# Sparse attention and a mixture of experts on one core: scores and products with v at two points of a unit's stretch in place of one

## The chip, the cores and the metric

The kernel runs on 1 core of one Trainium2 chip. The metric is the device time of one execution in microseconds (us).

## The reference

A batch of 4 sequences of 768 tokens with 8 heads of 64 passes through block-sparse attention (blocks of 32; each block of queries sees its neighbours, the first and last block, and 3 sampled blocks; the first and last block of queries see everything). Its output, 3072 tokens of 512, passes through a mixture of 4 experts.

```python
# attention
scores = scale * np.matmul(q, k.transpose(0, 1, 3, 2))
scores = np.where(mask, scores, -1000000000.0)
scores = scores - np.max(scores, axis=-1, keepdims=True)
attn = np.exp(scores)
attn = attn / (np.sum(attn, axis=-1, keepdims=True) + 1e-09)
out = np.matmul(attn, v)
# experts: x (3072, 512), w1 (4, 512, 1024), w2 (4, 1024, 512)
p = domain_probs / (domain_probs.sum(-1, keepdims=True) + 1e-09)
for e in range(E):
    h = np.maximum(x @ w1[e], 0.0)
    out += p[:, e:e + 1] * (h @ w2[e])
```

## The kernel before

Attention of batch 0 runs first, by itself. After that one stream of expert products (`experts()`, a generator) fills TensorE, and attention of batches 1, 2 and 3 ("later attention") is threaded into it: batch b's attention runs while the experts work on batch b-1. The experts go on after the last attention.

*The experts.* The four experts' hidden layers are 8 chunks of 512. Matrix products are made of seven smaller ones (the scheme of Strassen and Winograd; in batch 0 the second layer is plain). Each number is split in two fp32r parts, and three partial products give the accuracy of fp32. A first-layer product (`first`, `first7`, matmuls at L754, tiles `w` and `v`) is 6 matmuls of 128x128 by 128x384, and so is a second-layer product of the later batches (`second7`, L991, tiles `u` and `v`); batch 0's second layer (`second`, L827, tile `po`) has 3 matmuls of 128x512. Their results are taken out of PSUM by VectorE and ScalarE. Of these steps the text names L813, L842, L869, L892 and L902 (VectorE's sums and the scaling by the expert's weight `pb`, tile `ha`). The sum into the output tile `tot` is at L1001. `hidden` makes the second layer's operands: a cast on ScalarE (L914) and a subtraction on POOL (L915).

*Attention in units.* A batch has N = 16 units: 4 of kind Edge (first and last block of queries, each over two halves of the keys) and 12 of kind Group (6 groups of up to 4 query blocks, each for two halves of the heads). A unit has four steps:
- `S`: the scores, 32 or 64 small matmuls of 64x32 tiles (16 for an Edge; L355, L362 and L433, tiles `s` and `sw`) into two PSUM buffers, then on VectorE the mask and the row maximum (L372; for an Edge L444 to L449), and on ScalarE the exponential (L374; L451) into `p`;
- `T`: 6 or 8 transposes of `p` on TensorE (L383, L462) into the same two PSUM buffers that S uses, each half copied out to `pt` by ScalarE (L385, L463);
- `A`: the products with v, 32, 48 or 64 small matmuls of 128x32 tiles (L396, L474, tile `o`), then on VectorE the normalisation (L402 to L404 into `xg`; for an Edge L481 to L489 into `xe`);
- `X`: after every second unit, the transposes of the finished rows (L415, L495, tiles `x` and `xt`), in the one PSUM buffer that A uses too, and ScalarE's copy into the expert's input (L417, L497).

`copy_k` brings the sampled key blocks together (L158, POOL and ScalarE), `load_q` and `load_v` fetch q and v (SyncE's queue, and POOL's indirect loads at L213).

*The order.* It is written out by hand: each engine executes its instructions in the order in which the program issues them. `drive(until)` takes products from the stream until the sum of their planned costs (`T1` = 0.975 us for a 384-column product, `T2` = 0.6475 for one of batch 0's second layer) reaches `until`. Batch b's later attention has `N + 1` equal stretches of planned length `per` between two fixed points of the stream:

```python
LEAD, TAIL = 32.0, 25.0
start = base[b - 1] + LEAD
per = (base[b] - TAIL - start) / (N + 1)
```

With `base` of 0, 235.5, 440.2 and 660.6 this gives 10.5, 8.7 and 9.6 us of planned products for batches 1, 2 and 3. In stretch n, X of unit n-2 and T of unit n-1 come at the stretch's beginning, and S of unit n and A of unit n-1 together at its middle. At n = 0 there is S alone, at n = 16 A alone. The copies and loads for the next groups follow A.

Of the kernel before, what the change touches and what calls it, by code (L numbers as in the profile page):

```python
# [23 lines left out]
def attention_moe_kernel(ctx: ExitStack, tc, qb, kb, vr, sampled, sampled_t, probs, w1, w2, out):  # L24
# [60 lines left out]
    def load_batch(b):  # L85
        k = gp.tile([P, NB, P], F32, name="k", bufs=1)
        q = gp.tile([P, 2, P], F32, name="qe", bufs=1)
        for m in range(2):
            ns = slice(m * NB // 2, (m + 1) * NB // 2)
            nc.sync.dma_start(k[:, ns], kb[b, :, ns])  # L90
            if m == 0:
                nc.sync.dma_start(q, qb[b, :, 0:NB:NB - 1])
        vs = []
        if b == 0:
            whole = pool["v"].tile([P, KT, DM], F32, name="vn")
        for m in range(0, KT, 4):
            n = min(4, KT - m)
            if b == 0:
                v = whole[:, m:m + n]
            else:  # L100
                v = pool["v"].tile([P, 2, 2, DM], F32, name="v").rearrange("p a b e -> p (a b) e")
            nc.sync.dma_start(v[:, :n], vr[b * S + P * m:b * S + P * (m + n)]
                              .rearrange("(k p) e -> p k e", p=P))
            vs += [v[:, i] for i in range(n)]
        keys[b] = k, q, vs
# [4 lines left out]
    def load_q(b, t):  # L110
        js = blocks(t)
        q = gp.tile([P, QG, P], F32, name="q")
        nc.sync.dma_start(q[:, :len(js)], qb[b, :, js[0]:js[-1] + 1])
        gathered[b, t] = q, {}, {}
# [15 lines left out]
    def copy_k(b, t, cs=range(QG)):  # L130
        for c, j in enumerate(blocks(t)):
            if c in cs:
                odd = c % 2
                turn = kturn[odd]
                kturn[odd] = (turn + 1) % ((pool["nk"] + 1 - odd) // 2)
                key = pool["nk"], odd, turn

                full = b == 0
                if key not in ktiles:
                    ktiles[key] = [pool["k"].tile([P, SLOTS if full else SLOTS - 3, P], F32,  # L140
                                                  name=f"kr{odd}{turn}"), None]
                k, of = ktiles[key]
                kw = keys[b][0]
                at0 = 0 if odd or full else -3
                if of != b:
                    ktiles[key][1] = b
                    if odd:
                        nc.gpsimd.tensor_copy(k[:, NR:NR + 1], kw[:, NB - 1:NB])
                        nc.gpsimd.tensor_copy(k[:, NR + 1:NR + 2], kw[:, 0:1])
                    else:  # L150
                        nc.gpsimd.tensor_copy(k[:, 3 + at0:NR + 5 + at0:NR + 1], kw[:, 0:NB:NB - 1])
                if full:
                    nc.gpsimd.tensor_copy(k[:, odd * 5:odd * 5 + 3], kw[:, j - 1:j + 2])
                for r in range(NR):
                    eng = COPIERS[r % len(COPIERS)]
                    copy = eng.copy if eng is nc.scalar else eng.tensor_copy
                    to = r + (0 if odd else 4 + at0)
                    copy(k[:, to:to + 1], kw[:, bass.ds(sampled_block(j, r), 1)])  # L158
                gathered[b, t][1][c] = k
# [57 lines left out]
    def load_v(b, t, cs=range(QG)):  # L217
        js = blocks(t)
        for c in range(min(cs), min(max(cs) + 1, len(js)), 2):
            n = min(2, len(js) - c)  # L220
            v = pool["v"].tile([P, 2, 2, DM], F32, name="v")
            window(v, b, js[c:c + n])
            first_rows(v, b, n)
            for i in range(n):
                gather(v, b, i, js[c + i])
                gathered[b, t][2][c + i] = v[:, i]
# [276 lines left out]
    def units(b):  # L503
        return ([Edge(b, i, h) for i in range(2) for h in range(2)] +
                [Group(b, t, u) for t in range(NG) for u in range(2)])
# [10 lines left out]
    def conversion(b):  # L516

        b11, b12, b21, b22 = (xr[b][:, k * KH:(k + 1) * KH, g * HS:(g + 1) * HS]  # L520
                              for k in range(2) for g in range(2))

        def cast(n, src):
            xo[n] = (xp if n in (1, 2) else later["x"]).tile([P, 2, KH, HS], F32R, name=f"xo{n}")
            nc.scalar.copy(xo[n][:, 0], src)

        def rest(n, src, eng):
            eng.tensor_sub(xo[n][:, 1], src, f32(xo[n][:, 0]))

        cast(2, b21)  # L530
        yield
        rest(2, b21, nc.gpsimd)
        cast(1, b11)
        yield
        rest(1, b11, nc.gpsimd)
        yield
        cast(7, b12)
        yield
        rest(7, b12, nc.vector)
        cast(3, b22)  # L540
        yield
        if b:
            rest(3, b22, nc.gpsimd)
        nc.vector.tensor_sub(b11, b12, b11)
        if not b:
            rest(3, b22, nc.vector)
        yield
        cast(5, b11)
        yield
        rest(5, b11, nc.vector)  # L550
        nc.vector.tensor_sub(b11, b22, b11)
        yield
        cast(6, b11)
        nc.vector.tensor_sub(b12, b22, b12)
        yield
        rest(6, b11, nc.vector)
        nc.vector.tensor_sub(b21, b21, b11)
        yield
        cast(4, b21)
        yield  # L560
        rest(4, b21, nc.gpsimd)
        yield

        cast(7, b12)
        yield
        rest(7, b12, nc.vector)
        xr.pop(b)
        yield
# [551 lines left out]
    def drive(until):  # L1120
        while done[0] < until:
            done[0] += next(stream)[0]
# [3 lines left out]
    def spread_weights():  # L1126

        n = NT // P * E
        t = pool["a"].tile([P, P], F32, name="prt_ps", tag="a")
        nc.tensor.transpose(t[:n], pr.rearrange("p t e -> p (t e)"), ident)  # L1130
        rows = later["t"].tile([P, P], F32, name="prows", tag="t2", bufs=2)
        nc.scalar.copy(rows[:n], t[:n])
        nc.sync.dma_start(prt, rows[:n])
# [114 lines left out]
    for b in range(1, B):  # L1248
        us = units(b)
        start = base[b - 1] + LEAD  # L1250
        per = (base[b] - TAIL - start) / (N + 1)
        load_batch(b)
        load_q(b, 0)
        for n in range(N + 1):


            drive(start + n * per)
            if b == 1 and n == 0:
                spread_weights()
            if n > 1:  # L1260
                us[n - 2].X()
            if n > 0:
                us[n - 1].T(0)
                us[n - 1].T(1)
            drive(start + (n + 0.5) * per)
            if n < N:
                us[n].S()
            if n > 0:
                us[n - 1].A()
            if n == 1:  # L1270
                copy_k(b, 0)
                load_v(b, 0, (0, 1))
            t = (n - E0 + 2) // 2
            if n % 2 == 0 and 0 < t < NG:
                load_q(b, t)
                copy_k(b, t, (0,))
            elif n % 2 and 0 < t < NG:
                copy_k(b, t, (1, 2, 3))
                load_v(b, t, (0, 1))
            if n % 2 == 0 and 0 < t <= NG:  # L1280
                load_v(b, t - 1, (2, 3))
        drive(start + (N + 1) * per)
        us[N - 1].X()
        pieces[b] = conversion(b)
# [53 lines left out]
```

## Time and profile before

| | |
|---|---|
| median of 3 runs | 1234.09 us (1233.68 to 1235.0) |
| the profiled execution | 1232.82 us |
| its span in the profile | 1231.1 us |
| granted TensorE clock | 0.993 |
| TensorE busy, matmuls | 1189.1 us, 12243 of them |
| VectorE busy | 808.7 us |
| ScalarE busy | 519.8 us |
| POOL busy | 838.4 us |
| HBM | 264 GB/s over the span |

PE is TensorE's matmuls, PEld its weight loads, which overlap them; DVE is VectorE, ACT ScalarE, SP SyncE. A line such as L754 is a line of the kernel. Attention of batch 1 has its first S at 122.58 us and its last X at 366.36, batch 2 from 441.48 to 651.23, batch 3 from 718.83 to 942.80.

### The profile page before, as it was taken

What the parts mean: (1) busy time and instruction counts of PE and PEld (TensorE: products, weight loads), DVE (VectorE), ACT (ScalarE), POOL (GpSimd) and SP (SyncE); (2) the same over time, 40 slices, a digit from 0 to 9 for tenths busy, and PEclk for the clock granted to TensorE, in tenths of its full rate; (3) what the DMA queues carried; (4) which work ended last, traced back from release to release, by engine and by line L of the source; (5) the groups of instructions that cost most, each with busy time, mean ns of one, the idle gap of its engine ahead of it and who ended that gap; (6) DMA issues with size and microseconds to landing.
All of it is one profiled execution on the core that took longest, in us unless ns stands there. A gap on an engine that the chain in (4) does not pass through costs nothing.

```text
span 1231.1 us, 32030 instructions
## 1 busy us (share of the span) xinstructions
PE 1189.1 (97%) x12243; PEld 1095.4 (89%) x12243; DVE 808.7 (66%) x1701; ACT 519.8 (42%) x1259; POOL 838.4 (68%) x824
## 2 busy tenths in 40 slices
PE   7899999999999899999999999999999999999997
PEld 4678888888888898989989999989999999999997
DVE  4774757565654667767666867766566676666667
ACT  3864555656552243444533244444533333222221
POOL 7837978888776575767647775766755776666662
PEclk8999999999999899999999999999999999999999
DMA  9986869899979787888969786989876688887874
GB/s 289 264 281 232 312 246 351 290 316 318 307 266 351 227 242 233 259 278 274 270 211 345 227 267 222 286 252 283 285 253 209 219 271 266 258 262 251 255 239 154
DMA packets 214564, 326.81 MB, mean 265 GB/s; under 512 B 17483, under 2 KB 117420, under 8 KB 214412
## 3 DMA queue, kind: packets, MB, share of 16 engines
q1 hardware_dynamic: 207888, 303.53, 76.2%
q0 software_dynamic: 6480, 21.24, 5.8%
q8 instruction: 97, 1.59, 0.6%
q14 instruction: 55, 0.45, 0.1%
q10 hardware_dynamic: 44, 0.00, 0.0%
HBM read 257.02 MB, written 67.68 MB: 264 GB/s over the span
## 4 chain that ended last, share of the span: by engine, by line
PE 79%; DVE 5%; DMA 1%; issue 1%; ACT 1%; SPq 0%; POOL 0%; DVEq 0%; ACTq 0%
PE w L754 19%; PE u L991 15%; PE v L754 14%; PE v L991 12%; PE po L827 8%; PE o L396 3%; PE tp L383 2%; PE s L362 2%; PE s L355 1%; DVE ha L869 1%; PE x L415 1%; DMA pb<-prt 1%; DMA v<-in_vr_dram 1%; PE sw L433 1%; DVE tot L1001 1%
## 5 line engine op out<-in xcount | busy, mean ns | idle before, releaser
L915 POOL TENSOR_TENSOR ho<-ha,ho 128x768 fp32r<-128x768 f32 x165 | 318.3, 1938 | 244.8 <-ACT ho L914 242.0
L754 PE MATMUL w<-xo,wo 128*128 128x384 f32 x1524 | 310.9, 340 | 10.9 <-DVE ha L869 3.5
L754 PEld LDWEIGHTS w<-xo,wo 128*128 128x128 f32 x1524 | 268.8, 189 | 19.5 <-DVE ha L902 3.9
L914 ACT CAST ho<-ha 128x768 fp32r<-128x768 f32 x168 | 139.2, 837 | 269.9 <-DVE ha L869 106.1
L754 PE MATMUL v<-xo,wo 128*128 128x384 f32 x1176 | 238.9, 339 | 1.5 <-DVE xr L417 1.0
L991 PE MATMUL u<-ho,w2o 128*128 128x384 f32 x1128 | 228.2, 338 | 2.3 <-issue 2.3
L754 PEld LDWEIGHTS v<-xo,wo 128*128 128x128 f32 x1176 | 207.7, 189 | 6.4 <-DVE xr L417 1.1
L991 PEld LDWEIGHTS u<-ho,w2o 128*128 128x128 f32 x1128 | 197.0, 188 | 4.6 <-issue 2.9
L991 PE MATMUL v<-ho,w2o 128*128 128x384 f32 x888 | 179.8, 339 | 3.2 <-issue 1.5
L991 PEld LDWEIGHTS v<-ho,w2o 128*128 128x128 f32 x888 | 154.7, 188 | 7.1 <-DVE ha L869 2.7
L1001 DVE TENSOR_TENSOR tot<-v,tot 128x384 f32<-128x384 f32 x184 | 97.9, 552 | 91.6 <-PE v L991 90.3
L1001 DVE TENSOR_TENSOR tot<-u,tot 128x384 f32<-128x384 f32 x180 | 98.8, 552 | 47.9 <-PE u L991 47.8
L827 PE MATMUL po<-w2o,hh 128*128 128x512 f32 x384 | 123.5, 403 | 1.9 <-DVE oacc L842 1.9
L374 ACT ACTIVATE p<-p,mx 128x256 f32<-128x256 f32 (+1 forms) x192 | 95.3, 498 | 50.8 <-DVE mx L372 50.6
L213 POOL DMA_INDIRECT v<-in_vr_dram,vidx x81 | 79.9, 986 | 24.4 <-issue 17.8
L644 POOL TENSOR_TENSOR wo<-r,wo 128x256 fp32r<-128x256 f32 x92 | 72.4, 793 | 32.3 <-ACT wo L643 28.5
L372 DVE CUSTOM_DVE_ANT_1 p<-s,mask 128x256 f32<-128x256 f32 (+1 forms) x192 | 69.8, 419 | 22.0 <-PE s L362 17.0
L869 DVE SCALAR_TENSOR_TENSOR ha<-ha,pb 128x384 f32<-128x384 f32 x84 | 82.5, 982 | 0.0
L827 PEld LDWEIGHTS po<-w2o,hh 128*128 128x128 f32 x384 | 69.0, 188 | 12.6 <-DVE oacc L842 2.7
L827 PE MATMUL po<-w2o,hl 128*128 128x512 f32 x192 | 75.8, 395 | 0.0
L396 PEld LDWEIGHTS o<-v,pt 128*32 128x32 f32 x2816 | 46.1, 110 | 18.5 <-issue 13.5
L396 PE MATMUL o<-v,pt 128*32 128x64 f32 x2816 | 54.6, 221 | 5.1 <-issue 3.1
(169 smaller groups left out, 1627.3 us busy)
## 6 DMA issues: line engine op xcount, KB each, us to landing
w2o<-kept SPq DMA_DIRECT2D x168, 512.0 KB
wo<-kept SPq DMA_DIRECT2D x318, 256.0 KB
kept<-wo SPq DMA_DIRECT2D x106, 256.0 KB
v<-in_vr_dram SPq DMA_DIRECT2D x88, 192.0 KB
kept<-w2o SPq DMA_DIRECT2D x32, 512.0 KB
r<-in_w_dram SPq DMA_DIRECT2D x16, 512.0 KB
r<-in_w_dram SPq DMA_DIRECT2D x32, 256.0 KB
kept<-t SPq DMA_DIRECT2D x32, 256.0 KB
```

Source lines behind the costliest of these rows:

```text
L213: nc.gpsimd.indirect_dma_start(out=v[:, i, 1 - i], out_offset=None, in_=vr, element_offset=b * S * DM, in_offset=bass.IndirectOffsetOnAxis ...
L372: nc.vector.tensor_tensor_reduce(p.rearrange("p (a b) -> p a b", b=BLOCK), s[h][:n, i], mk, -SCALE, 3.0e38, ALU.add, ALU.min, mx[:n])
L374: nc.scalar.activation(p, p, AF.Exp, bias=mx[:n], scale=-1.0, accum_out=self.sums[:n, m:m + 1])
L396: nc.tensor.matmul(o[cs, m], self.pt[:, 2 * m + k, cs], vs[c][:, k, e], start=k == 0, stop=k == 1)
L644: nc.gpsimd.tensor_sub(o[:, 1], src, f32(o[:, 0]))
L754: nc.tensor.matmul(ps, w[:, wi, t], x[:, xi, t], start=fresh and m == 0, stop=m == 3 * KH - 1, skip_group_check=not fresh)
L827: nc.tensor.matmul(p, a[:, js], w[:, i], start=f == 0 and n == 0, stop=f == FT - 1 and n == 2)
L869: nc.vector.scalar_tensor_tensor(block(g, half), src, 0.0, q, op0=ALU.max, op1=ALU.mult)
L914: nc.scalar.copy(o[:, 0], src)
L915: eng.tensor_sub(o[:, 1], src, f32(o[:, 0]))
L991: nc.tensor.matmul(ps, w[:, j, wi, ds], h[:, hi, j], start=fresh and m == 0, stop=m == 5, skip_group_check=not fresh)
L1001: nc.vector.tensor_add(t, ps, t)
```

## The change

S of unit n is issued after a third of the stretch, and A of unit n-1, with the copies and loads that follow it, after two thirds. Nothing else differs.

```diff
@@ -1262,9 +1262,10 @@
             if n > 0:
                 us[n - 1].T(0)
                 us[n - 1].T(1)
-            drive(start + (n + 0.5) * per)
+            drive(start + (n + 1 / 3) * per)
             if n < N:
                 us[n].S()
+            drive(start + (n + 2 / 3) * per)
             if n > 0:
                 us[n - 1].A()
             if n == 1:
```

## The prediction

> **What bounds the kernel now.** I read the page first: the busy shares, then the chain that ended last.
>
> ```profile
> span 1231.1 us, 32030 instructions
> PE 1189.1 (97%) x12243; PEld 1095.4 (89%) x12243; DVE 808.7 (66%) x1701; ACT 519.8 (42%) x1259; POOL 838.4 (68%) x824
> PE 79%; DVE 5%; DMA 1%; issue 1%; ACT 1%; SPq 0%; POOL 0%; DVEq 0%; ACTq 0%
> ```
>
> TensorE (PE) is busy for 97% of the span and makes 79% of the chain; no other engine reaches 70% busy. It takes its instructions in order, so the time is the sum of the distances from each group of matmuls to the next, and a change counts by what it adds to that sum or takes from the waits in it. The second view is therefore the waits of TensorE in the three stretches in which later attention runs: 120 to 380 us (batch 1), 430 to 660 (batch 2), 710 to 950 (batch 3). Columns: who waited for whom, total in us, times, longest.
>
> ```profile
> PE po L827 <- DVE oacc L842: 1.9, 2, 1.0
> PE w L754 <- DVE z L813: 1.5, 2, 1.3
> PE o L396 <- DMA v<-in_vr_dram: 1.1, 1, 1.1
> ...
> PE w L754 <- DVE ha L902: 1.6, 1, 1.6
> PE w L754 <- DVE ha L892: 1.3, 1, 1.3
> PE v L991 <- DVE ha L869: 0.9, 2, 0.6
> ...
> PE w L754 <- DVE ha L902: 1.6, 1, 1.6
> PE xt L495 <- DVE xe L489: 0.7, 1, 0.7
> ```
>
> They sum to 4.5, 3.8 and 2.3: 10.6 us in all three stretches. That is all that better spacing of attention can give back, 0.9% of the time.
>
> The third view is TensorE's timeline. Columns: start, us, engine, line, operation, output and inputs, count. I use starts alone, since ends are modelled. First one unit as it is now, scores (S) and then products with v (A):
>
> ```profile
> 512.87 1.20 PE L754 MATMUL v<-xo,wo 128*128 128x384 f32 x6
> 513.91 1.21 PE L991 MATMUL v<-ho,w2o 128*128 128x384 f32 x6
> 515.04 0.40 PE L355 MATMUL s<-k,q 64*32 64x96 f32 x16
> ...
> 516.18 1.10 PE L396 MATMUL o<-v,pt 128*32 128x64 f32 x64
> 517.21 1.31 PE L754 MATMUL w<-xo,wo 128*128 128x384 f32 x6
> 518.36 0.86 PE L991 MATMUL u<-ho,w2o 128*128 128x384 f32 x4
> ```
>
> An expert product followed by another takes 513.91 - 512.87 = 1.04 us. The one before S takes 515.04 - 513.91 = 1.13, S 1.14, A 1.03, and the product after A 518.36 - 517.21 = 1.15. So this visit costs, beyond its own matmuls, 0.09 when the stream leaves products and 0.11 when it comes back.
>
> **The change, part by part.** No instruction is added or removed. S of unit n moves from the middle of its stretch to a third, A of unit n-1 to two thirds, with what follows A (copies of sampled keys, loads of q and v). In the plan's own units a third of a stretch is 3.5, 2.9 and 3.2 us for batches 1, 2 and 3 (the stretches are 10.5, 8.7 and 9.6 by the formula in the code) and a product 0.975, so two or more products always come between S and A: the split really happens. It happens where both exist, n = 1 to 15, in three batches: 45 times.
>
> *The split on TensorE.* One visit becomes two. Batch ends already hold the halves: at n = 0 there is S without A, at n = 16 A without S. An S alone, then an S with A (both of the edge kind, 16 matmuls), then an A alone:
>
> ```profile
> 440.35 1.21 PE L754 MATMUL v<-xo,wo 128*128 128x384 f32 x6
> 441.48 0.88 PE L433 MATMUL sw<-k,qe 64*32 64x384 f32 x16
> 442.29 1.33 PE L991 MATMUL v<-ho,w2o 128*128 128x384 f32 x6
> 443.45 1.22 PE L754 MATMUL w<-xo,wo 128*128 128x384 f32 x6
> ...
> 452.60 0.88 PE L433 MATMUL sw<-k,qe 64*32 64x384 f32 x16
> 453.40 0.88 PE L474 MATMUL ow<-v,ptw 128*32 128x64 f32 x48
> 454.21 1.31 PE L754 MATMUL v<-xo,wo 128*128 128x384 f32 x6
> ...
> 643.67 1.20 PE L754 MATMUL w<-xo,wo 128*128 128x384 f32 x6
> 644.81 1.09 PE L396 MATMUL o<-v,pt 128*32 128x64 f32 x32
> 645.83 1.31 PE L991 MATMUL u<-ho,w2o 128*128 128x384 f32 x6
> 646.97 1.20 PE L754 MATMUL w<-xo,wo 128*128 128x384 f32 x6
> ```
>
> S takes 0.81 when a product follows (441.48 to 442.29) and 0.80 when A follows, so S gains nothing by losing A behind it. The product after the lone S takes 443.45 - 442.29 = 1.16, which is 0.12 over 1.04. The product before the lone A takes 644.81 - 643.67 = 1.14, 0.10 over. These two are new for every split (the entry to S and the exit from A are paid already): 0.22 us x 45 = 9.8 us, all of it in TensorE's order, where nothing covers it. For the weight loads, the same place reads (in brackets the idle time before):
>
> ```profile
> 516.18 0.94 PEld L396 LDWEIGHTS o<-v,pt 128*32 128x32 f32 x64 [0.25 <-issue]
> 644.81 0.93 PEld L396 LDWEIGHTS o<-v,pt 128*32 128x32 f32 x32 [0.25 <-issue]
> ```
>
> The load into A idles 0.25 us for nothing that the profile shows, whether S stood before it or a product: the tile's shape changes there (64x32 or 128x128 to 128x32).
> The Trainium skill, "TensorEngine Tiling (Array Packing)", section Tiling Modes, says that a change of the tiling mode, not of the tile alone, drains the array; the trace agrees with its 0.25 us, and since S, A and products have three modes, a unit that changed mode three times would do so four times. By that rule with the gap's 0.25 us as the price of one more drain, the sum would take 45 x 0.25 = 11.3 us in place of 9.8.
> I keep 0.22, since starts of matmuls are what adds up.
>
> *What S and A leave on VectorE.* VectorE is in order too. The longest waits come where both bursts stand ahead of the evacuation that a product waits for, as here:
>
> ```profile
> 799.41 0.42 DVE L372 CUSTOM_DVE_ANT_1 p<-s,mask 128x256 f32<-128x256 f32 x1
> ...
> 800.78 0.91 DVE L402 TENSOR_SCALAR rec<-sums 128x4 f32<-128x4 f32 x1
> 801.73 0.18 DVE L403 RECIPROCAL rec<-rec 128x4 f32<-128x4 f32 x1
> 802.01 0.42 DVE L404 TENSOR_TENSOR xg<-o,rec 128x256 f32<-128x256 f32 x1
> 802.35 0.55 DVE L902 TENSOR_TENSOR ha<-w,ha 128x384 f32<-128x384 f32 x1
> ...
> 802.95 1.31 PE L754 MATMUL w<-xo,wo 128*128 128x384 f32 x6 [1.63 <-DVE ha L902]
> ```
>
> S's reductions hold the queue from 799.41 to 800.78, A's normalisation (L402 to L404) to 802.35, and L902 comes last. With A one or two products later, L402 to L404 (0.91 + 0.18 + 0.42 = 1.5 us) fall behind L902. I take back 1.5 us at each of the two L902 waits (3.0), half of L892's 1.3 (0.65), 0.6 of L869's 0.9, half of batch 1's 4.5 (2.25, since there POOL and DMA set the pace and either end is possible): 6.5 us, of at most 10.6 and at least 0. Late next is the other half: a burst at two places meets twice as many tight products, each with S's 1.4 us or A's 1.5 instead of 2.9.
>
> *New shortages.* Each of these has less room than now, from about half a stretch to a third. (a) S needs the two PSUM buffers that the transposes (T) use, so ScalarE must have copied them out. (b) X, the transpose of a finished group, needs A's normalisation. (c) The key copies come later while the next S comes earlier. The rows:
>
> ```profile
> 504.23 1.46 POOL L158 COPY kr<-k 128x128 f32 x6
> ...
> 510.84 1.07 ACT L385 COPY pt<-tp 128x512 f32<-128x512 f32 x2
> ...
> 747.90 1.70 DVE L482 SCALAR_TENSOR_TENSOR rec<-rec,edge 128x2 f32<-128x2 f32 x1
> ...
> 750.21 1.32 DVE L489 TENSOR_TENSOR xe<-eo,rec 128x128 f32<-128x128 f32 x1
> ```
>
> (a) The copies end at 511.91, S starts at 515.04: 3.1 us of room; one or two products earlier leaves 1.0 to 2.1, so no wait except where ScalarE is late. (b) For edges, L482 and L489 are stretched to 1.70 and 1.32, and the page of waits shows X already 0.7 late once; there are six such X, and with a product or two less of room (1.0 to 2.1 us), but S's burst no longer ahead of A's, I bound them by 0 and 6 us. (c) The keys are there at 505.7, 9.3 us before S at 515.04; even 4.2 us less leaves 5. In the queues, what the stream issues between the middle and two thirds now goes ahead of A's followers: on SyncE the weight reloads of one or two products pass the loads of q and v, on POOL at most an operand split passes the copies and gathers, on ScalarE a cast passes its key copies. The loads of v keep a whole stretch to their A, because both move by the same sixth; ready work behind A there starts at most two products later. I take 2 us for all of this, nearer to 0 than to 6, as only one X of six is late today.
>
> *Sum:* 9.8 - 6.5 + 2.0 = +5.3 us. The profiled execution took 1232.82 us (span 1231.1 and 1.7 around it), the median of the runs is 1234.09, 1.3 higher and within their spread. I add the sum to the median: 1239.4 us.
>
> **The rivals.**
> 1. *Faster: the pause between S and A goes with the split.* Point: if S followed by a product takes 0.25 us less than S followed by A, each split costs 0.22 - 0.25 = -0.03 us, -1.4 us in all; with -6.5 + 2.0 that is -5.9, 1228.2 us. For it: the 0.25 us gap ahead of A's loads. Against it: S lasts 0.81 and 0.80 in the two cases, and the lone A has the same gap. It decides as soon as a split costs under 0.1 us (45 x 0.1 = 4.5, what the waits give).
> 2. *No change: all the waits go.* -10.6 us against 9.8: -0.8, 1233.3 us. For it: most of the waits are of evacuations that stand behind S and A on VectorE. Against it: 1.1 us is a DMA and 0.7 an X that gets less room.
> 3. *The waits only move.* Two bursts in two places, X later, T's copies late: 3 us returned and 5 lost, +11.8, 1245.9 us. For it: TensorE's product order has a VectorE evacuation to wait for about once per stretch, and the rooms under (a) and (b) shrink. Against it: each burst is half as long.
>
> **How the numbers follow.** My own case 0.60, rival 1 0.06, rival 2 0.14, rival 3 0.20. A run of this kernel tells 0.2% (2.5 us) from no change. Slower by more than that holds my case but for its low edge, and rival 3: 0.60 x 0.95 + 0.20 = 0.77; same: 0.14 plus that edge 0.03 = 0.17; faster 0.06. The range goes from just above rival 2 to rival 3: 1234.0 to 1246.5, which leaves out rival 1 and the far ends of 2 and 3.
>
> **What the changed profile would show.** The split: S followed by a product in every unit, that product 1.16 us long, the product before A 1.14, both 0.10 to 0.12 over 1.04, and 45 more idle gaps of 0.25 us ahead of weight loads. The return: no wait of a product for L902 behind L402 to L404, and the three sums 4.5, 3.8 and 2.3 falling to about 2, 1.5 and 1 before new ones. The new shortages: waits of `xt` or `x` for VectorE, of `s` for ScalarE's L385. The prediction is wrong if a lone S lets its product start early (rival 1), if a split's cost lies in places where TensorE would have waited anyway, or if the waits of the three stretches sum to more than now.

## The result, and the profile after

| | before | changed |
|---|---|---|
| median | 1234.68 us (6 runs, 1233.68 to 1236.18) | 1244.43 us (6 runs, 1242.45 to 1248.13) |
| profiled execution | 1232.82, span 1231.1 | 1242.45, span 1240.4 |

The change makes the kernel slower: ratio 1.0082, 95% interval 1.0064 to 1.0100, that is +9.7 us where +5.3 was forecast; the time is inside the range. Run again with the last experiments, it was slower by 1.0103 (1.0086 to 1.0119), +12.5 us. The page of the changed kernel, its lines on the span and on busy time:

```profile
span 1240.4 us, 32039 instructions
PE 1198.2 (97%) x12243; PEld 1094.3 (88%) x12243; DVE 808.1 (65%) x1701; ACT 520.2 (42%) x1259; POOL 838.2 (68%) x824
```

The counts of matmuls and of the vector instructions are the same, and so is the busy time of DVE, ACT and POOL within 0.6 us. TensorE alone is busy 9.1 us longer, with the same matmuls. Its timeline shows one unit of batch 2 (start, us, engine, line, operation):

```profile
519.71 1.21 PE L754 MATMUL v<-xo,wo 128*128 128x384 f32 x6
520.85 0.40 PE L355 MATMUL s<-k,q 64*32 64x96 f32 x16
...
521.99 1.31 PE L991 MATMUL v<-ho,w2o 128*128 128x384 f32 x6
523.13 1.20 PE L754 MATMUL w<-xo,wo 128*128 128x384 f32 x6
524.17 1.20 PE L991 MATMUL u<-ho,w2o 128*128 128x384 f32 x6
525.30 1.10 PE L396 MATMUL o<-v,pt 128*32 128x64 f32 x64
526.34 1.31 PE L754 MATMUL v<-xo,wo 128*128 128x384 f32 x6
```

By starts: S 521.99 - 520.85 = 1.14 and A 526.34 - 525.30 = 1.04 (before 1.14 and 1.03). The product after S takes 523.13 - 521.99 = 1.14, the one before A 525.30 - 524.17 = 1.13, an undisturbed one 1.04. Those are the two new terms, 0.10 and 0.09 in this unit. Over all units of later attention the medians are 0.106 after S and 0.095 before A: 0.20 us for each split, 45 x 0.20 = 9.0 us.

The weight loads at the same place pause on the way into S, on the way into A, and now also on the way back from S to the products (in brackets the idle time before, where it is over 0.2 us):

```profile
520.84 0.18 PEld L355 LDWEIGHTS s<-k,q 64*32 64x32 f32 x16 [0.25 <-issue]
521.98 0.99 PEld L991 LDWEIGHTS v<-ho,w2o 128*128 128x128 f32 x6 [0.25 <-issue]
525.30 0.94 PEld L396 LDWEIGHTS o<-v,pt 128*32 128x32 f32 x64 [0.25 <-issue]
526.33 0.99 PEld L754 LDWEIGHTS v<-xo,wo 128*128 128x128 f32 x6
```

Each split has one such pause more than a unit had before, as forecast. The last row has none: back from A to the products, also a change of the tile's shape, the loads idle 526.33 - 526.24 = 0.09 us.

TensorE's waits in the three stretches of later attention (120 to 390, 430 to 670, 710 to 960 us; total, times, longest):

```profile
PE w L754 <- DVE z L813: 3.0, 1, 3.0
PE o L396 <- DMA v<-in_vr_dram: 1.7, 1, 1.7
PE w L754 <- DVE hl L773: 1.0, 1, 1.0
...
PE xt L495 <- DVE xe L489: 0.9, 2, 0.7
PE v L754 <- ACT ha L894: 0.5, 1, 0.5
PE w L754 <- DVE ha L902: 0.4, 1, 0.4
PE x L415 <- DVE xg L404: 0.3, 1, 0.3
...
PE xt L495 <- DVE xe L489: 1.5, 1, 1.5
PE x L415 <- DVE xg L404: 0.3, 1, 0.3
```

They sum to 5.7, 2.1 and 1.8, where before they were 4.5, 3.8 and 2.3: 9.6 us against 10.6. The 0.5 for L894 is not new: before the change the same wait, 0.48 us, stands at 425.68 us, just outside the stretch that begins at 430. Like with like it is 9.1 against 10.6, 1.5 us returned. In batches 2 and 3 the old waits are nearly gone (L902 3.2 to 0.4, L892 1.3 to 0, L869 0.9 to 0), and new ones of X stand in their place (0.7 to 3.0). In batch 1 they grew.

One cost stands in no list of waits. Behind the wait of 3.0 us for L813 the granted TensorE clock in the changed profile is 0.50 for 3.4 us, from 159.6 to 163.0 us; behind the wait of 1.3 us at the same place before the change it stays at 1.00. The product that waited and the next one of its kind, first before, then changed:

```profile
156.77 1.31 PE L754 MATMUL w<-xo,wo 128*128 128x384 f32 x6 [1.33 <-DVE z L813]
...
159.30 1.29 PE L754 MATMUL v<-xo,wo 128*128 128x384 f32 x6
...
158.92 1.76 PE L754 MATMUL w<-xo,wo 128*128 128x384 f32 x6 [3.03 <-DVE z L813]
...
163.04 1.29 PE L754 MATMUL v<-xo,wo 128*128 128x384 f32 x6
```

The same matmuls take 159.30 - 156.77 = 2.53 us before and 163.04 - 158.92 = 4.12 in the changed kernel: 1.6 us on top of the longer wait.

### The profile page after: what moved, and what is told of

Read it like the earlier page. It is cut to its first block, busy times and chain, and to the rows that moved or that the text cites. A ratio compares the mean times of both kernels' runs of the same rounds, so it can differ in the third digit from the quotient of the medians.

```text
span 1240.4 us, 32039 instructions
## 1 busy us (share of the span) xinstructions
PE 1198.2 (97%) x12243; PEld 1094.3 (88%) x12243; DVE 808.1 (65%) x1701; ACT 520.2 (42%) x1259; POOL 838.2 (68%) x824
## 4 chain that ended last, share of the span: by engine, by line
PE 78%; DVE 4%; DMA 3%; issue 1%; SPq 1%; POOL 1%; ACT 0%; DVEq 0%; ACTq 0%
PE w L754 19%; PE u L991 15%; PE v L754 14%; PE v L991 12%; PE po L827 8%; PE o L396 3%; PE tp L383 2%; PE s L362 2%; DMA v<-in_vr_dram 1%; PE s L355 1%; DMA kept<-r 1%; DVE ha L869 1%; DMA pb<-prt 1%; PE sw L433 1%; PE x L415 1%
## 5 line engine op out<-in xcount | busy, mean ns | idle before, releaser
L754 PE MATMUL w<-xo,wo 128*128 128x384 f32 x1524 | 312.8, 341 | 10.1 <-DVE ha L869 4.3
L754 PEld LDWEIGHTS w<-xo,wo 128*128 128x128 f32 x1524 | 268.3, 189 | 22.5 <-issue 7.3
L754 PE MATMUL v<-xo,wo 128*128 128x384 f32 x1176 | 239.0, 339 | 1.5 <-DVE xr L417 1.0
L991 PE MATMUL u<-ho,w2o 128*128 128x384 f32 x1128 | 229.3, 339 | 2.3 <-issue 2.3
L754 PEld LDWEIGHTS v<-xo,wo 128*128 128x128 f32 x1176 | 206.9, 188 | 7.8 <-issue 1.5
L991 PEld LDWEIGHTS u<-ho,w2o 128*128 128x128 f32 x1128 | 196.5, 188 | 7.5 <-issue 5.7
L991 PE MATMUL v<-ho,w2o 128*128 128x384 f32 x888 | 180.1, 339 | 2.3 <-issue 1.5
L991 PEld LDWEIGHTS v<-ho,w2o 128*128 128x128 f32 x888 | 154.5, 188 | 7.0 <-issue 3.5
L644 POOL TENSOR_TENSOR wo<-r,wo 128x256 fp32r<-128x256 f32 x92 | 72.6, 794 | 39.1 <-ACT wo L643 35.0
L869 DVE SCALAR_TENSOR_TENSOR ha<-ha,pb 128x384 f32<-128x384 f32 x84 | 69.7, 830 | 0.0
L396 PEld LDWEIGHTS o<-v,pt 128*32 128x32 f32 x2816 | 46.6, 110 | 20.4 <-issue 15.8
L396 PE MATMUL o<-v,pt 128*32 128x64 f32 x2816 | 55.1, 221 | 6.9 <-issue 4.2
```

The source lines that it names most:

```text
L396: nc.tensor.matmul(o[cs, m], self.pt[:, 2 * m + k, cs], vs[c][:, k, e], start=k == 0, stop=k == 1)
L644: nc.gpsimd.tensor_sub(o[:, 1], src, f32(o[:, 0]))
L754: nc.tensor.matmul(ps, w[:, wi, t], x[:, xi, t], start=fresh and m == 0, stop=m == 3 * KH - 1, skip_group_check=not fresh)
L869: nc.vector.scalar_tensor_tensor(block(g, half), src, 0.0, q, op0=ALU.max, op1=ALU.mult)
L991: nc.tensor.matmul(ps, w[:, j, wi, ds], h[:, hi, j], start=fresh and m == 0, stop=m == 5, skip_group_check=not fresh)
```

## The experiments

Theory 1: the time is the price of a split on TensorE, wherever S and A stand, and the waits are a second, smaller term. Theory 2: the split is cheap, and the new places of S and A make waits. All ratios are to runs of the kernel before on the same chip, with 95% intervals.

**One product between S and A.** S stays at the middle.

```diff
             if n < N:
                 us[n].S()
+            if 0 < n < N:
+                done[0] += next(stream)[0]
             if n > 0:
                 us[n - 1].A()
```

> S stays at the middle of its stretch and A follows it after one expert product, so all 45 visits are split with hardly any move. Theory 1 (the price is the split itself, 0.22 us of TensorE's order each): 45 x 0.22 = 9.8 us slower, within 2 us, and 45 products after S of 1.14 to 1.16 us. Theory 2 (the split is cheap, the time comes from waits that the new places of S and A make): at most 3 us slower, since S hasn't moved and A by one product alone.

Measured: 1.0051 (1.0033 to 1.0070), +5.8 us by medians: more than theory 2 allows, less than theory 1's price. The timeline has the whole price in one product, the one between S and A: 516.13 - 514.89 = 1.24, 0.20 over 1.04.

```profile
513.75 0.40 PE L355 MATMUL s<-k,q 64*32 64x96 f32 x16
...
514.89 1.31 PE L754 MATMUL w<-xo,wo 128*128 128x384 f32 x6
516.13 1.10 PE L396 MATMUL o<-v,pt 128*32 128x64 f32 x64
517.16 1.31 PE L991 MATMUL u<-ho,w2o 128*128 128x384 f32 x6
```

Forty-five times 0.20 is 9.0. What is missing from it came back in waits, which theory 1 had left unchanged. First batch 1, then 441 to 965 us:

```profile
PE w L754 <- DVE z L813: 1.1, 2, 1.0
PE po L827 <- DVE oacc L842: 0.6, 1, 0.6
...
PE o L396 <- issue: 2.8, 6, 0.5
PE xt L495 <- DVE xe L489: 1.1, 2, 0.7
```

The waits for other engines are 2.8 us in place of 10.6. The 2.8 us with no releaser ("issue") are six short pauses inside A; a kernel without a split has such pauses too (1.2 us with S and A both at two thirds). Together 9.0 - 7.8 + 2.8 = 4.0 us, at the lower end of the measured 4.1 to 8.6.

**A in two halves with one product between them.** S and the first half stay together.

```diff
             for m in range(2 * HH):
+                if m == HH and between:
+                    between()            # done[0] += next(stream)[0]
                 e = slice((2 * HH * u + m) * D, (2 * HH * u + m + 1) * D)
```

> S and A stay together at the middle, but A is cut in two halves (two of a Group's four heads, or one of an Edge's two, each) with one expert product between them; same matmuls, one normalisation after the second half. Theory 1 (each further visit costs 0.22 us): 45 x 0.22 = 9.8 us slower, within 2 us, although S and A are not parted. Theory 2 (the cost comes from parting S from A): no more than 3 us slower.

Measured: 1.0064 (1.0042 to 1.0086), +8.8 us. So an additional visit costs without S and A being parted. The product between the halves is again 0.20 longer (median). The agreement with 9.8 is partly luck: each half of A costs more than half (0.58 x 2 = 1.17 against 1.03), which adds some 6 us, and waits of about as much came back.

**S, a product, half of A, a product, half of A.** The two edits above in one.

> S, one expert product, the first half of A, one expert product, the second half of A: 90 visits more than before in place of 45. Theory 1 (each visit costs 0.20 us of TensorE's order): 18 us of splits, less at most some 8 us of waits that the kernels with 45 gave back, so 10 to 18 us slower, and 45 x 0.20 = 9 us above the kernel with one product between S and A (6.3) and the one with A in halves (7.9), within 3: about 16. Theory 2 (the waits set the price): no more than 8 us slower.

Measured: 1.0177 (1.0159 to 1.0194), +21.8 us, above the expected 16. Here is one unit (L398 is L396, L758 is L754, L995 is L991):

```profile
516.23 0.40 PE L355 MATMUL s<-k,q 64*32 64x96 f32 x16
...
517.37 1.31 PE L995 MATMUL v<-ho,w2o 128*128 128x384 f32 x6
518.61 0.65 PE L398 MATMUL o<-v,pt 128*32 128x64 f32 x32
519.19 1.31 PE L758 MATMUL w<-xo,wo 128*128 128x384 f32 x6
520.43 0.65 PE L398 MATMUL o<-v,pt 128*32 128x64 f32 x32
521.02 1.31 PE L995 MATMUL u<-ho,w2o 128*128 128x384 f32 x6
```

Both products in between take 1.24 us. Ninety times 0.20 is 18, and A's halves (0.58 and 0.59 against 1.03) add 6: 24 us, of which the waits gave some back. Theory 2's "no more than 8" is out.

**S and A together at a third, and together at two thirds.** Only the 0.5 is replaced.

> S and A stay together, moved to a third of the stretch. Theory 1 (the split is the price, the place is not): no split price, so within 3 us of before. Theory 2 (the places make the waits): slower by 4 us or more here or in the kernel with both at two thirds, the two together reaching the 9.7 us of the change.

> S and A stay together, moved to two thirds of the stretch. Theory 1: within 3 us of before, with more waits of X and T, which come sooner after. Theory 2: slower by 4 us or more here or in the kernel with both at a third.

Measured: 1.0013 (0.9998 to 1.0029) at a third, 0.9979 (0.9965 to 0.9994) at two thirds: +0.8 and -2.6 us. Neither place costs anything near 9.7 us while S and A stay together, so the cost needs the split. Once S and A are parted, the places matter too: with the same 45 splits the kernel with one product between them was 5.8 us slower, the change 9.7 and 12.5, and the waits returned 7.8 us there and 1.5 here. The waits do move: at a third one wait of 2.4 us of an Edge's S for the copies of T appears, which is the shortage that the prediction listed under (a).

```profile
PE sw L433 <- ACT ptw L463: 2.4, 1, 2.4
```

**The change in batch 1 alone, and in batches 2 and 3 alone.**

```diff
-            drive(start + (n + 0.5) * per)
+            drive(start + (n + (1 / 3 if b == 1 else 0.5)) * per)
             if n < N:
                 us[n].S()
+            if b == 1:
+                drive(start + (n + 2 / 3) * per)
```

> Places at a third and two thirds in batch 1 alone; batches 2 and 3 as before. The whole change took 9.7 us. If batch 1's waits grow with the change, as the ends of the attentions in the two profiles suggest (batch 1's last X came 6.6 us later, batch 2's 0.9 more, batch 3's 2.0 more): 15 splits (3.3 us) and 3.3 us of waits, 6.6 us slower, within 1.5 us. If the waits of that one profile were chance: 3.3 us, within 1.

> Places at a third and two thirds in batches 2 and 3, batch 1 as before. If these two batches get waits back: 30 splits (6.5 us) less about 3.5 us, 3 us slower, within 1.5 us. If nothing came back: 6.5 us slower, within 1.

Measured: 1.0058 (1.0035 to 1.0082), +7.8 us, for batch 1 alone; 1.0050 (1.0030 to 1.0070), +6.0 us, for the others (the condition turned round). By medians batch 1, with 15 of the 45 splits, pays the larger part, though the intervals overlap. Its waits are the same as in the whole change, so they were not chance:

```profile
PE w L754 <- DVE z L813: 3.1, 1, 3.1
PE o L396 <- DMA v<-in_vr_dram: 2.2, 1, 2.2
PE w L754 <- DVE hl L773: 0.9, 1, 0.9
```

6.2 us, against 4.5 before. Fifteen splits (3.0 us) and 1.7 us of waits are 4.7 of the 7.8 measured (4.3 to 10.1). The profile also has a pause of 2.0 us without a releaser in batch 3, where nothing was changed; the rest is open. For batches 2 and 3 the measured 6.0 is nearer to 6.5 (nothing came back) than to 3, but the profile shows that waits did come back: the named ones of these two batches fell from 6.1 to 3.4 us, and pauses without a releaser inside S and A, 2.5 us, used that up (30 x 0.20 - 2.7 + 2.5 = 5.8). The two parts add up to 13.8, above the 9.7 of the first measurement and near the 12.5 of the second.

**Only the normalisation later.** S and A stay together; L402 to L404 and L481 to L489 become a step `R` of their own, issued one product after A and its copies and loads, or at two thirds.

```diff
             if n > 0:
-                us[n - 1].A()
+                us[n - 1].A(True)                  # matmuls alone
...
+            if n > 0:
+                done[0] += next(stream)[0]         # or: drive(start + (n + 2 / 3) * per)
+                us[n - 1].R()                      # the normalisation
```

> S and A together at the middle as before; only A's normalisation on VectorE (L402 to L404, L481 to L489) is issued one expert product later. No further visit of TensorE. Theory 1 (split price and waits are two separate terms): no split price, and the waits fall as they did in the profile of the kernel that has one product between S and A (10.6 us in the three stretches to 2.9), 7.7 us faster, 4 to 8. Rival (the waits that a profile shows are made up elsewhere): within 2 us of before.

> S and A together at the middle; A's normalisation at two thirds of the stretch. Theory 1: no split price; the waits for L902, L892 and L869 go as in the changed kernel, but X finds its rows late as there (3.0 us in batches 2 and 3, L489 and L404), so less is gained than with one product: 2 to 5 us faster. Rival: within 2 us of before.

Measured: one product later 0.9972 (0.9956 to 0.9989), 4.0 us faster; at two thirds 1.0030 (1.0014 to 1.0045), 3.1 us slower, where 2 to 5 faster was expected. So the return is real, without a split to pay for it, if the normalisation moves by no more than it must. The named waits of the first (441 to 965 us; its lines are 15 further down, L917 is L902, L504 is L489, L884 is L869):

```profile
PE xt L510 <- DVE xe L504: 0.7, 1, 0.7
PE w L769 <- DVE ha L917: 0.3, 1, 0.3
PE v L1006 <- DVE ha L884: 0.3, 1, 0.3
```

1.3 us in place of 6.1; batch 1 stayed at 5.3 against 4.5. In all 6.6 in place of 10.6, the 4.0 us that were measured; the expected 7.7 failed in batch 1. At two thirds X finds its rows late in all three batches; batch 1, then the others (L422 is L415, L413 is L404):

```profile
PE xt L510 <- DVE xe L504: 2.8, 1, 2.8
...
PE x L422 <- DVE xg L413: 3.0, 2, 1.5
```

**Batch 1 at a third, the others with the late normalisation.** No split anywhere.

```diff
-            drive(start + (n + 0.5) * per)
+            drive(start + (n + (1 / 3 if b == 1 else 0.5)) * per)
...
+                us[n - 1].A(b > 1)
...
+            if n > 0 and b > 1:
+                done[0] += next(stream)[0]
+                us[n - 1].R()
```

> S and A together everywhere: in batch 1 at a third of the stretch, in batches 2 and 3 at the middle with the normalisation one product later. No further visit. The waits in the profiles of the kernels that had one of the two: batch 1 2.4 us (from 4.5), batches 2 and 3 0.3 and 1.0 (from 3.8 and 2.3). If they add up: 6.9 us faster; the kernel with the late normalisation alone was 3.5 us faster, so 3.5 to 7.

Measured: 0.9955 (0.9939 to 0.9971), 1229.73 us against 1234.69, 5.0 us faster: the fastest kernel of this study. Its named waits are 2.4 us in batch 1 and 2.1 in the others, 4.5 in place of 10.6.

**The transposes in two halves.** A visit whose tile has the products' shape.

```diff
                 us[n - 1].T(0)
+                done[0] += next(stream)[0]
                 us[n - 1].T(1)
```

> S and A as before; the transposes T are cut in two halves with one expert product between them, so 48 more visits that leave the products and come back, but T's tile is 128x128 as the products' is. If the price of a visit is the change of the tile's shape: the product before T stays at 1.04 us, and the only extra is that the product after the first half takes 1.13 as it does after T now (0.09 us), 48 x 0.09 = 4.3 us slower, within 2.5. If any further visit costs the full 0.20: 9.6 us slower.

Measured: 1.0042 (1.0027 to 1.0057), +5.6 us. The rows:

```profile
509.80 1.21 PE L991 MATMUL v<-ho,w2o 128*128 128x384 f32 x6
510.84 0.60 PE L383 MATMUL tp<-ident,p 128*128 128x128 f32 x4
511.19 1.30 PE L754 MATMUL w<-xo,wo 128*128 128x384 f32 x6
512.33 0.60 PE L383 MATMUL tp<-ident,p 128*128 128x128 f32 x4
512.68 1.29 PE L991 MATMUL u<-ho,w2o 128*128 128x384 f32 x6
```

The product before T takes 510.84 - 509.80 = 1.04: no price for leaving. The one between the halves takes 512.33 - 511.19 = 1.14: 0.10 for coming back (0.09 by the median of all units), although no shape changes. So of the 0.20 us of a split only the 0.095 before A can be put down to the change of shape; most of what follows a visit comes also after short matmuls of the products' own shape. T's matmuls are longer than A's, 128 columns against 64, and no run separates that from the shape. In T's case half of the price is given back, since the halves take 0.35 each and the whole 0.79 (some halves are shorter, and give less): 48 x 0.09 = 4.3, less 2.2. By these rows the kernel should be some 2 us slower; it is 5.6 (3.3 to 7.0), and what makes up the rest is open. Its one profile has a pause of 2.5 us without a releaser in batch 3, and behind it 3.4 us at a granted clock of 0.50, in which two products take 1.80 and 1.85 us.

**The whole change again.**

> The whole change again, beside the others on one chip: 9.7 us slower as before, within 2. Theory 1's terms: 45 x 0.20 = 9.0 us of splits and the rest waits.

Measured: 1.0103 (1.0086 to 1.0119), +12.5 us, just above the expected span. Its named waits are those of the first profile within 0.2 us, but its span is 4.2 us longer (1244.6 against 1240.4). Of these, 1.2 us stand already at the first S of batch 1 (121.28 against 120.09 us), before any of the splits. Another 1.4 come behind A's wait for v at 266 us: there the granted clock is 0.50 for 3.4 us in this profile and 1.00 in the first, and the matmuls from the wait's end to the second product behind it take 271.81 - 265.99 = 5.82 us against 268.92 - 264.54 = 4.38. The products after S are slightly longer (median 0.119 over in place of 0.106; 0.2 us in all). Why these vary between executions is open.

## Why the prediction was right, step by step

- *The split on TensorE:* right. 0.22 us was read from the lone S and the lone A at the ends of batches; 0.20 was measured in the changed kernel, 9.0 us in place of 9.8 (45 x 0.22 is 9.9; the slip has no weight). Three other ways to add visits showed the same 0.20 on the product in between. The Trainium skill's rule in "TensorEngine Tiling (Array Packing)", section Tiling Modes, that a change of tiling mode drains the array, agrees with the pauses of 0.25 us into S, out of S and into A; out of A, also a change of mode, the loads idle only 0.09 us. The transposes in halves show that a change of mode can account for only about half of the price.
- *What S and A leave on VectorE:* right in mechanism for batches 2 and 3. L902's waits gave 2.8 of the 3.0 taken, L892's 1.3 (0.65 taken), L869's 0.9 (0.6). The step that failed is the half of batch 1's 4.5 us (2.25) that was taken back without a row for it: batch 1 lost 1.2 us. L842's 1.9 us did go, but the wait for L813 grew from 1.3 to 3.0, L773 brought 1.0, and v's DMA 0.6 more. L813 stands behind an Edge's normalisation (from L481 on) in both kernels, so that order is not what changed. VectorE before, then in the changed kernel:

```profile
148.66 0.95 DVE L637 TENSOR_TENSOR r<-s,r 128x256 f32<-128x256 f32 x1
...
154.10 0.15 DVE L481 TENSOR_TENSOR rec<-edge,ew 128x2 f32<-128x2 f32 x1
...
156.17 0.55 DVE L813 TENSOR_TENSOR z<-w,z 128x384 f32<-128x384 f32 x1
...
151.24 0.95 DVE L637 TENSOR_TENSOR r<-s,r 128x256 f32<-128x256 f32 x1 [2.28 <-POOL wo L644]
...
156.89 0.15 DVE L481 TENSOR_TENSOR rec<-edge,ew 128x2 f32<-128x2 f32 x1
...
158.32 0.54 DVE L813 TENSOR_TENSOR z<-w,z 128x384 f32<-128x384 f32 x1
```

  L637 (a sum for the experts' weights) starts 2.6 us later and L813 2.2, while TensorE's last product ahead of these rows stands only 0.3 us later (147.07 against 146.81). L637 waits for POOL's L644, and POOL reaches that L644 only after the key copies and gathers that follow A, whose last ends at 149.75 in place of 146.03 us. That is the shift in POOL's queue that the prediction named among the new shortages and took as small. It is read from this one place. It fits that the normalisation at two thirds, with the copies behind A as before, left this wait at 1.3 us.
- *The clock:* the sum had no term for it. The longer wait for L813 was followed by 3.4 us at a granted clock of 0.50, which cost 1.6 us.
- *New shortages:* 2.0 us taken; the waits of X in batches 2 and 3 grew by 2.3 (0.7 to 3.0). It was (b), X after A, as named. No wait of S for (a) or (c) showed; the queues' order showed in batch 1.
- *The sum:* 9.8 - 6.5 + 2.0 = +5.3 became 9.0 for the splits, -1.5 for the named waits of the three stretches (10.6 to 9.1), 0.8 for a wait between batches 1 and 2 that the stretches leave out (L754 for L869, 3.5 to 4.3), and 1.6 at the lower clock: +9.9, of the 9.3 us between the two spans. So the direction and the price of the split were understood, and the -4.5 for everything else was not: it came to about +0.3. That the time still lay inside the range is partly luck, for the range reached up to it only to take in rival 3.
- *The rivals:* 1 (the pause between S and A goes) is refuted by the rows: S takes 1.14 with either follower. 2 (all waits go) nearly happened with one product between S and A, and was still slower. 3 (the waits only move) came closest to the whole.

## What to carry to other kernels

Where one in-order engine is full, count how often its work changes kind, and take the price of leaving and returning from places where the trace already has each half alone. A wait that two bursts cause together can often be removed by moving the part that runs on the other engine (here the normalisation, by one product) and leaving the full engine's order as it is. Don't take back half of a stretch's waits because either end is possible: without a row for the new order the middle is no estimate. Where a wait of the full engine grows, look also at the granted clock behind it; here it cost nearly as much (1.6 us) as the growth of the wait (1.7).

## What the runs showed of the hardware that was not expected

A product after a visit is 0.09 to 0.11 us longer, even when the visit's tile has its own shape (T). Half a burst of 128x32 matmuls takes 0.58 us where the whole takes 1.03, but half of T 0.35 where the whole takes 0.79: cutting made A's burst 0.14 us longer and T's 0.09 shorter.

Behind the wait of 3.0 to 3.1 us for L813 the granted clock fell to 0.50 for 3.4 us in both profiles of the changed kernel, but not in the kernel with the change in batch 1 alone, whose wait there was 3.1 us as well. What decides it no run shows; it is a part of why single profiles of one kernel differ by several us.
